# Second convolution of a residual block: a unit's two outer rows placed next to each other, odd weight regions moved by 528 elements

## The chip, the cores and the metric

The kernel runs on one core of a Trainium2 chip. The metric is the device time of one execution in microseconds (us), and lower is better. A run list gives the time of several executions; the profile describes one execution of its own.

## What is computed

A residual block of a diffusion network for two images of 512 channels and 64 x 64 pixels. Two 3 x 3 convolutions with 512 inputs and 512 outputs hold nearly all of the work:

```python
h = conv3(_silu(gn(x, g1, be1)), w1)
emb = _silu(t_emb) @ w_emb
h = h + emb.reshape(B, C, 1, 1)
h = conv3(_silu(gn(h, g2, be2)), w2)
return x + h
```

`gn` is a group norm over four groups of 128 channels. `conv3` pads by one pixel and sums nine taps, each a 512 x 512 product over the channels. Inputs and output are bf16; the kernel keeps intermediate data in fp16.

## The kernel before

**Units.** Each convolution is cut into chunks: an image (`b`) and half of its rows (`ch`), so four chunks for the first convolution (c = 0 to 3) and four for the second (c = 4 to 7). In a chunk, each of the four tiles of 128 output channels (k = 0 to 3) is one unit. Units are numbered 0 to 31; units 16 to 31 are the second convolution, and units 28 to 31 are its last chunk, c = 7.

**A unit's work.** The rows are transformed so that four output rows come from six row planes, s = 0 to 5 (function `rows_a`, `rows_b` and `prod` make the planes of the next chunk while a chunk is multiplied). Planes 0 to 3 are the inner ones; they are also transformed along the columns and multiplied in two kinds of matmul, `B_mms` and `A_mms`. Planes 4 and 5 are the outer ones. In chunks 4 to 6 they are multiplied by `plain_mms` with the three column taps as they are (matmuls with 512 moving columns); in units 28 to 30 they are multiplied by `C_mms` and `D_mms` (256 columns), for which `outer_weights` (L757) first makes sums and differences of the taps on VectorE. TensorE's results go to PSUM, ScalarE copies them to SBUF (`evac_m`, `evac_b`, and `evac_o` at L838 for the outer planes), VectorE combines the inner planes into four output rows in a buffer `ys`, and the two outer rows are added to the first and last of these. There are two `ys` buffers, for even and odd units.

**How the outer rows are added.** In units 16 to 27 an accumulating DMA issued by GpSimd (POOL) adds them (L1034 to L1038, called the accumulate here): one DMA with two runs of 520 elements per partition, one from each outer row, except that units 16 and 17 use two DMAs of one run each. After it, a second POOL DMA adds the whole of `ys` to the output in HBM (called the output DMA here), to which the input `x` has been copied earlier.

**Where things lie.** One big SBUF tile `ar` holds everything. Its first part is four regions `UREG[0]` to `UREG[3]` of 10,256 elements each. In the second convolution region j holds, from its start, 8,192 elements of inner weights of output tile j (`um1`, L509, filled by `fetch_w2`, L594), then at 8,192 a streamed part of 1,536 elements, then at 9,728 one outer row of 520 elements. The streamed part belongs to no fixed tile: a unit u uses slot s = u mod 2, which is the pair of regions 2s and 2s + 1, and its raw outer weights are loaded in two halves, channels 0 and 1 of the input into region 2s and channels 2 and 3 into region 2s + 1 (`stream_w2`, L605; `st_off`, L512). I call these the even half and the odd half; each is a DMA of 384 KB. The unit's two outer rows lie in the same two regions:

```python
OO = [UREG[2 * (u % 2) + 1] + 9728, UREG[2 * (u % 2)] + 9728]
...
oo = A(OO[1], [[OO[0] - OO[1], 2], [1, PL]])
```

So the accumulate's source (L1028) is one access pattern with two runs, 10,256 elements apart.

**What sets the order.** Every operation is recorded by a planner and then emitted in the order of a fixed list (`ORDER`, `emit`), so each engine and each DMA queue has one fixed order. SyncE (SP) issues all plain loads and stores (helper `dma`, L385), in order: a load that waits holds all that stand behind it. POOL issues the accumulates, the output DMAs and some small memsets, in order as well. The planner knows the exact elements of each access. The waits that the chip sees are not the planner's: the framework below adds them when the operations are emitted, from the access patterns of the one tile `ar`. In the built program of before, the odd half of a unit's streamed weights (nine of the sixteen odd halves) waits for an accumulate of an earlier unit of the same slot, and nine accumulates wait for an odd half that was loaded; the even halves have no such wait, although they lie next to an outer row in the same way.

**The place that matters below.** SP issues, in this order: the odd half of unit 27 and some more; then the odd half of unit 28, its even half, the even half of unit 29, a part of `x` for the last unit, the odd half of unit 29; later the even and odd halves of units 30 and 31. The odd half of unit 28 waits for the accumulate of unit 26, of unit 24, and for the last matmul of unit 26 that reads the old odd half. VectorE reads the new half in `outer_weights`.

All vector additions are recorded by one helper and stand under L347, scalings on VectorE under L351, ScalarE's work under L370, matmuls under L400 and DMAs under L385.

Of the kernel before, what the change touches and what calls it, by code (L numbers as in the profile page):

```python
# [14 lines left out]
BF16 = mybir.dt.bfloat16  # L15
# [100 lines left out]
def _idx(off, dims):  # L116
    idx = np.array([off])
    for s, c in dims:
        idx = (idx[:, None] + (np.arange(c) * s)[None, :]).reshape(-1)
    return idx  # L120
# [3 lines left out]
RW = 65  # L124
# [13 lines left out]
CFG = {  # L138
    'k0': ('DVE', 'DVE', 'DVE', 'DVE'),
    't0': 'DVE',  # L140
    'k': ('DVE', 'DVE', 'DVE', 'ACT', 'ACT', 'ACT', 'DVE', 'ACT'),
    't': ('DVE', 'DVE', 'DVE', 'DVE', 'ACT', 'ACT', 'ACT', 'DVE'),
    's': (('DVE', 'DVE', 'DVE'), ('DVE', 'DVE', 'DVE'), ('DVE', 'ACT', 'ACT'), ('DVE', 'DVE', 'DVE'), ('ACT', 'ACT', 'ACT'), ('ACT', 'ACT', 'DVE'), ('ACT', 'ACT', 'ACT'), ('DVE', 'ACT', 'DVE')),
    'st1': (1, 1, 1, 1),
    'oacc': (4, 4, 4, 0, 4, 4, 4, 0),
    'ym': (1, 1),
# [14 lines left out]
    'embat': -1,  # L161
    'aacc': (0, 0, 0, 0, 0, 0, 0, 0),
    'embk': 1,
}


# [54 lines left out]
def kernel(  # L221
# [15 lines left out]
    UREG, UM = [], 10256  # L237
# [57 lines left out]
    def K(*k):  # L295
        if k not in keys:
            keys[k] = len(keys)
        return ("K", np.array([keys[k]]))

    def A(off, dims, dt=None):  # L300
        b = ar[:] if dt is None else ar[:].bitcast(dt)
        n = 1
        for d in dims:
            n *= d[1]
            assert d[1] == 1 or -32768 <= d[0] <= 32767
        return R(bass.AP(b.tensor, b.offset + off, [list(b.ap[0])] + [list(d) for d in dims]),
                 ("A", _idx(off, dims)), n)
# [35 lines left out]
    def regs(*rs):  # L343
        return [r.reg if isinstance(r, R) else r for r in rs]

    def tt(out, a, b, op, name=""):
        pl.op("DVE", 0.075 + 0.000521 * out.n, lambda: nc.vector.tensor_tensor(out=out.ap, in0=a.ap, in1=b.ap, op=op),  # L347
              regs(a, b), regs(out), name)
# [31 lines left out]
    def dma(out, in_, r, w, nbytes, name="", sw=False, acc=False, after=None, seq=None):  # L380
        rate = 0.15 if acc else rate0[0]
        kw = {"accum_op": ALU.add, "max_dma_last_dim": 2080} if acc else {}
        eng = nc.gpsimd if sw else nc.sync
        return pl.op("DMA", nbytes / rate * 1e-6 if nbytes > 30000 else 0.1,
              lambda: eng.dma_start(out=out, in_=in_, **kw), regs(*r), regs(*w), name, lat=3.2 if sw else None, after=after, sw=sw, seq=seq)  # L385

    def memz(eng, out, name="", v=0.0):
        e = getattr(nc, eng)
        pl.op("POOL" if eng == "gpsimd" else "DVE", 0.08 + 0.0005 * out.n, lambda: e.memset(out.ap, v), (), regs(out), name)  # L389
# [116 lines left out]
    def ur0(j, ct, ky, kx):  # L506
        return A(UREG[j] + 7168 + ct * 768 + ky * 384 + kx * 128, [[1, 128]], BF16)

    def um1(j, ct, kx, pos):  # L509
        return A(UREG[j] + ct * 2048 + kx * 512 + pos * 128, [[1, 128]])  # L510

    def st_off(s, ct):  # L512
        return UREG[2 * s + ct // 2] + 8192 + (ct % 2) * 768

    rawc = [0]

# [76 lines left out]

    def fetch_w2(j):  # L594
        nm = f"f2_{j}"
        d = A(UREG[j], [[2048, 4], [1, 1536]])
        dma(d.ap, u_scr[j], [K("u", j, c) for c in range(CT)], [d], P * 4 * 3072, nm)
        for c in range(0, CT, 2):
            g = lambda kx: A(UREG[j] + c * 2048 + kx * 512, [[2048, 2], [1, 512]])
            t = A(TB, [[512, 2], [1, 512]])  # L600
            tt(t, g(0), g(2), ALU.add, nm)
            tt(g(3), t, g(1), ALU.add, nm)
            tt(g(1), t, g(1), ALU.subtract, nm)

    def stream_w2(s, j):  # L605
        for h in range(2):
            d = A(UREG[2 * s + h] + 8192, [[1, 1536]], BF16)
            dma(d.ap, w2[j][:, h * 1536:(h + 1) * 1536], [], [d], P * 3072, f"st_{j}")


# [2 lines left out]
    def nst(c):  # L613
        return CFG["nst"][c] if c < 4 else 4
# [142 lines left out]
    def outer_weights(sl, k):  # L757
        nm = f"ow{k}"
        for h in range(2):
            g = lambda kx: A(UREG[2 * sl + h] + 8192 + kx * 128, [[384, 4], [1, 128]], BF16)  # L760
            t = A(VB[0] + 6144 + h * 512, [[1, 512]])
            cd = ND[k] + h * 1024
            tt(t, g(0), g(2), AD, nm)
            tt(A(cd, [[1, 512]]), t, g(1), AD, nm)
            tt(A(cd + 512, [[1, 512]]), t, g(1), SB_, nm)
# [48 lines left out]
    def unit(c, k, opening=0):  # L814
        l, b, ch = chunks[c]
        md = mode(c)
        u = ucnt[0]
# [5 lines left out]
        M = lambda i, n=1, st=512: A(MB + i * 512, [[st, n], [1, 512]]) if n > 1 else A(MB + i * 512, [[1, 512]])  # L823
        if md == "1":
            BT, SD = BT1, SD1
            OO = [UREG[2 * (u % 2) + 1] + 9728, UREG[2 * (u % 2)] + 9728]
        else:
            BT, SD = BT0, SD0
            OO = [O0[2 if u == 2 else u % 2] + PL, O0[2 if u == 2 else u % 2]]
        if l == 0 and ch == 0 and b not in SSUM:  # L830
# [7 lines left out]
        def evac_o(s, bank):  # L838
            act(A(OO[s - 4], [[RW, 8], [33, 2], [1, 32]]), Ps(bank, 0, [[1, 512]]), fid,
                scale=(0.25, 1.0)[s - 4], acc=acc(s), name=nm + f"o{s}")  # L840
# [118 lines left out]
        elif c == 7 and CFG["no"]:  # L959
# [13 lines left out]
            g = lambda q: A(NB_ + q * 256, [[512, 2], [32, 8], [1, 32]])  # L973
# [39 lines left out]
        if last:  # L1013
# [6 lines left out]
            for r0, n, i in ((1, 2, None), (3, 1, 0), (0, 1, 1)):  # L1020
                if i is not None:
                    tt(seg(ot, r0, 1, BF16), seg(ys, r0, 1), A(OO[i], [[1, PL]]), AD, nm + "O")
                o_ = seg(ot, r0, n, BF16)
# [3 lines left out]
        yo = A(ys, [[24 * RW, 2], [1, PL]])  # L1027
        oo = A(OO[1], [[OO[0] - OO[1], 2], [1, PL]])  # L1028
        if c == 7 and CFG["no"]:
            for i in range(2):  # L1030
                yr = A(ys + i * 24 * RW, [[RW, 8], [33, 2], [1, 32]])
                tt(yr, yr, A(NB_ + 2560 - i * 512, [[1, 512]]), AD, nm + "O")
        elif k < CFG["oacc"][c] and c == 4 and k < 2:
            for i in range(2):  # L1034
                y_, o_ = A(ys + 24 * RW * i, [[1, PL]]), A(OO[1 - i], [[1, PL]])
                dma(y_.ap, o_.ap, [o_, y_], [y_], P * 2 * PL, nm + "oa", sw=True, acc=True)
        elif k < CFG["oacc"][c] and not last:
            dma(yo.ap, oo.ap, [oo, yo], [yo], P * 4 * PL, nm + "oa", sw=True, acc=True)  # L1038
        else:
            tt(yo, yo, oo, AD, nm + "O")  # L1040
# [157 lines left out]
    for ct in range(CT):  # L1198
        d = A(XB0[ct], [[1, AF]], BF16)
        dma(d.ap, x[0, ct, 0], [], [d], P * AF * 2, f"x0{ct}", seq=seq)  # L1200
        d = A(XB1[ct], [[1, YF]], BF16)
# [69 lines left out]
    for c in range(8):  # L1271
        l, b, ch = chunks[c]
        for k in range(CT):
            if c == 0:
                if k + 1 < CT:
                    if k == 2:
                        load_ur(3)
                    prep_w1(k + 1, "ACT", [WS, E0[0], E0[1], TB])
                if k == CFG["embk"]:
                    emb()  # L1280
            if c == CFG["np"]:
                nest_w1(k)
            if c < 4 and nst(c) == 3 and nst(c - 1) != 3:
                nest_w1b(k)
            for i in range(CFG["w2d"][c][k]):
                prep_w2(w2n[0] // 4, w2n[0] % 4)
                w2n[0] += 1
            if c == 4 and k == 0:
                for j in range(CT):
                    memz("gpsimd", A(UREG[j] + 9728 + 32, [[RW, 8], [1, 1]]), "oz")  # L1290
            if l == 1:
                stream_w2(ucnt[0] % 2, k)
                if c == 7 and k < 3 and CFG["no"]:
                    outer_weights(ucnt[0] % 2, k)
                for i in range(2 if ucnt[0] < 31 else 0):
                    r0, r1 = i * YF // 2, (i + 1) * YF // 2
                    dma(out[b, k, ch][:, r0:r1], x[b, k, ch][:, RW + r0:RW + r1], [], [K("o", b, k, ch, i)],
                        P * YF * 1.4, f"pre{c}{k}", after=ufirst[max(ucnt[0] - CFG["pre"], 0)])
            run_later = list(later)
            later.clear()  # L1300
            unit(c, k, opening=2 if c == 0 and k < 3 else 0)
            for f in run_later:
                f()
            if c == 0:
                stats1(k)
            if c == 1:
                if k == CFG["st1at"]:
                    gn_chain(0, 1, 0, [(ME1, 0, 2 * CT)], "st1", n=CT)
                for q in range(CT):
                    if k == max(CFG["st1at"], min(q + CFG["st1at"], CT - 1)):  # L1310
                        prod(2, q)
            elif c + 1 < 8:
                prod(c + 1, k)
            if c == 3:
                fetch_w2(k)
# [71 lines left out]
```

## Time and profile before

| what | us |
| --- | --- |
| median of 3 runs (lowest to highest) | 467.13 (466.95 to 468.02) |
| the profiled execution, its time | 466.26 |
| the profiled execution, its span | 464.5 |
| TensorE (PE) matmuls busy | 447.6 (96% of the span) |
| VectorE (DVE) busy | 440.9 (95%) |
| ScalarE (ACT) busy | 377.0 (81%) |
| GpSimd (POOL) busy | 65.8 (14%) |

The span is the time from the first to the last instruction of the program in the trace; the profiled execution's own time is 1.76 us longer. Two engines are busy for nearly all of the span, so an average says little: what counts is where either of them stands still. A line of the timeline reads: start, length, engine, source line, operation, what is written and read, how many instructions are merged into the line, and in square brackets the idle time before it and what ended that. A line of the waits reads: engine, what was waited for, the sum of the time, the number of waits, the longest. SPq is SP's queue of DMA issues. The granted clock (PEclk) is 1.00 when TensorE runs at full speed. DMAs of the profile's list of issues are given with the time from issue to landing.

### The profile page before, as it was taken

The page shows a single profiled execution, that of the slowest core. Times are in us where ns is not written, and L with a number is a line of the kernel's source. Part 1 is how long each engine was busy: PE and PEld are TensorE (multiplying, and loading weights), DVE is VectorE, ACT ScalarE, POOL GpSimd, SP SyncE. Part 2 cuts the span into 40 slices and gives each one's busy share as a digit, 9 for nine tenths or more (in the row PEclk, how much of TensorE's full clock was granted, in tenths as well). Part 3 has the DMA queues.
Part 4 walks back from the last instruction along what each step waited for, and adds up shares of the span by engine and source line. Part 5 has one row for each costly group of instructions (what it writes and reads, how often), then busy time and mean ns, then how long its engine had stood idle before and what let it go on. Part 6 is the DMA issues. An engine that isn't in the chain of part 4 may idle for free. (4 is left out here: it accounts for less than half of the span.)

```text
span 464.5 us, 8112 instructions
## 1 busy us (share of the span) xinstructions
PE 447.6 (96%) x2891; PEld 281.5 (61%) x2891; DVE 440.9 (95%) x842; ACT 377.0 (81%) x571; POOL 65.8 (14%) x91
## 2 busy tenths in 40 slices
PE   8999999999999999999999999999999999959995
PEld 5744344465554666566556766657776677747882
DVE  4899999999999999999999999999999999949995
ACT  5899999987958999998999898757868798726572
POOL 2210010211021111011000002122221231211210
PEclk9999999999999999999999999999999999998999
DMA  8955682697649387686977687779789777495744
GB/s 314 381 215 168 177 220 71 179 270 212 216 103 295 85 254 230 190 254 198 355 263 275 213 290 177 187 188 195 184 215 268 215 173 180 70 222 136 163 76 92
DMA packets 44472, 94.89 MB, mean 204 GB/s; under 512 B 6544, under 2 KB 18192, under 8 KB 44432
## 3 DMA queue, kind: packets, MB, share of 16 engines
q1 hardware_dynamic: 32208, 77.60, 49.4%
q0 software_dynamic: 11936, 16.78, 23.5%
q8 instruction: 22, 0.36, 0.3%
q14 instruction: 18, 0.15, 0.1%
q10 hardware_dynamic: 288, 0.01, 0.0%
HBM read 62.25 MB, written 31.32 MB: 201 GB/s over the span
## 5 line engine op out<-in xcount | busy, mean ns | idle before, releaser
L400 PE MATMUL psum<-ar 128*128 128x256 f16 (+2 forms) x2771 | 429.7, 317 | 9.6 <-ACT ar L370 5.4
L347 DVE TENSOR_TENSOR ar<-ar 128x1040 f16<-128x1040 f16 (+8 forms) x621 | 409.0, 716 | 12.6 <-DMA ar<-in_w_dram 6.5
L400 PEld LDWEIGHTS <-ar 128*128 128x128 f16 (+1 forms) x2763 | 269.0, 98 | 166.8 <-issue 14.9
L370 ACT ACTIVATE ar<-psum 128x512 f16<-128x512 f32 (+4 forms) x250 | 158.9, 679 | 42.6 <-DVE ar L347 21.9
L370 ACT ACTIVATE ar<-ar 128x512 f16<-128x512 f16 (+6 forms) x146 | 158.9, 1116 | 31.3 <-DVE ar L347 26.6
L370 ACT ACTIVATE ar<-ar,fs 128x2112 f16<-128x2112 bf16 (+1 forms) x32 | 68.8, 2150 | 4.3 <-DVE fs L497 1.9
L385 POOL DMA_DIRECT2D ar<-ar x35 | 38.7, 1126 | 196.6 <-DVE ar L347 80.8
L351 DVE TENSOR_SCALAR ar<-ar 128x512 f16<-128x512 f16 (+3 forms) x90 | 31.4, 370 | 0.4 <-issue 0.2
L385 POOL DMA_DIRECT2D out_dram<-ar x15 | 19.0, 1266 | 55.1 <-DMA ar<-ar 30.0
L370 ACT ACTIVATION_READ_ACCUMULATOR ar<-psum 128x1 f32 x104 | 22.3, 214 | 0.0
L389 POOL MEMSET ar<- 128x65 f16 (+4 forms) x29 | 5.3, 216 | 116.0 <-DVE ar L347 76.8
L400 PEld LDWEIGHTS <-ones_bf 128*128 128x128 bf16 x75 | 7.5, 105 | 6.2 <-issue 3.7
L400 PE MATMUL psum<-ar,ones_bf 128*128 128x260 bf16 x56 | 7.3, 275 | 0.7 <-DMA ar<-in_x_dram 0.7
L400 PE MATMUL psum<-ones_bf 128*128 128x512 bf16 x19 | 6.8, 501 | 1.1 <-DVE ones_bf L404 1.1
L370 ACT ACTIVATION_READ_ACCUMULATOR ar<-ar 128x1 f32 x36 | 7.3, 202 | 0.0
L478 POOL TENSOR_TENSOR fs<-fs 128x1 f32<-128x1 f32 x4 | 3.7, 915 | 17.9 <-DVE fs L476 17.9
L400 PEld LDWEIGHTS psum<-fs,ones_neg 128*128 128x128 f32 x36 | 4.7, 191 | 1.6 <-ACT ar L370 1.0
L400 PE MATMUL psum<-fs,ones_neg 128*128 128x1 f32 (+3 forms) x36 | 4.7, 242 | 0.4 <-ACT ar L370 0.4
L400 PE MATMUL psum<-ar,s_sb 128*2 128x512 bf16 x9 | 2.7, 377 | 0.0
L438 ACT ACTIVATE s_sb<-tparm 128x18 bf16<-128x18 bf16 x1 | 0.2, 219 | 3.0 <-DMA tparm<-in_t_emb_dram 3.0
L432 ACT ACT_TABLE_LOAD x1 | 1.3, 1283 | 1.7 <-PEq L1371 1.7
L437 DVE CAST fs<-gparm 128x16 f32<-128x16 bf16 x1 | 0.2, 174 | 2.5 <-DMA gparm<-in_params_dram 2.5
(54 smaller groups left out, 25.5 us busy)
## 6 DMA issues: line engine op xcount, KB each, us to landing
ar<-in_w_dram SPq DMA_DIRECT2D x36, 384.0 KB, 4.4
ar<-in_x_dram SPq DMA_DIRECT2D x16, 552.5 KB, 4.4
h_scr<-ar SPq DMA_DIRECT2D x16, 520.0 KB, 3.8
ar<-h_scr SPq DMA_DIRECT2D x16, 520.0 KB, 4.4
ar<-ar POOLq DMA_DIRECT2D x31, 260.0 KB, 4.5
out_dram<-in_x_dram SPq DMA_DIRECT2D x30, 260.0 KB, 5.3
out_dram<-ar POOLq DMA_DIRECT2D x15, 520.0 KB, 7.2
ar<-in_x_dram SPq DMA_DIRECT2D x13, 520.0 KB, 6.3
```

The source lines that it names most:

```text
L347: pl.op("DVE", 0.075 + 0.000521 * out.n, lambda: nc.vector.tensor_tensor(out=out.ap, in0=a.ap, in1=b.ap, op=op), regs(a, b), regs(out), name)
L351: pl.op("DVE", cost or 0.075 + 0.00026 * out.n, lambda: nc.vector.tensor_scalar(out=out.ap, in0=a.ap, scalar1=s, scalar2=None, op0=ALU.mul ...
L370: lambda: nc.scalar.activation(out=out.ap, in_=a.ap, func=func, scale=sc, **kw), regs(*rr), regs(*ww), name)
L385: lambda: eng.dma_start(out=out, in_=in_, **kw), regs(*r), regs(*w), name, lat=3.2 if sw else None, after=after, sw=sw, seq=seq)
L389: pl.op("POOL" if eng == "gpsimd" else "DVE", 0.08 + 0.0005 * out.n, lambda: e.memset(out.ap, v), (), regs(out), name)
L400: nc.tensor.matmul(out.ap, lhsT=lhsT.ap, rhs=rhs.ap, start=st, stop=sp, skip_group_check=True)
L432: nc.scalar.activation(out=fs[:, WARM:WARM + 1], in_=fs[:, WARM + 1:WARM + 2], func=ACT.Silu)
L437: nc.vector.tensor_copy(out=fs[:, GB:GB + 4 * CT], in_=gparm[:])
L438: nc.scalar.activation(out=s_sb[:], in_=tparm[:], func=ACT.Silu)
L478: pl.op("POOL", 0.85, lambda: nc.gpsimd.tensor_tensor(out=F(rs, n).ap, in0=N.ap, in1=F(NEGH, n).ap, op=ALU.pow), regs(N), regs(F(rs, n)), ...
```

## The change

Odd regions (j = 1 and 3) are laid out the other way around: the outer row comes first, at the region's start, and the inner weights and the streamed part follow 528 elements on. Region 2s still ends with its outer row, at 9,728 to 10,248, and region 2s + 1 begins at 10,256, so the two outer rows of a slot now lie 528 elements apart in place of 10,256, with 8 elements between them and nothing of another kind in between. The two runs of the accumulate, its bytes and its addresses in `ys` stay. All weight addresses of odd regions go through `um_off`; the zeroing of a pad column of the outer rows follows the new place. A constant in the condition of the split accumulates becomes an entry of the table with the same value.

```diff
+    'split4': 2,
...
+    def um_off(j):
+        return UREG[j] + 528 * (j % 2)
+
     def um1(j, ct, kx, pos):
-        return A(UREG[j] + ct * 2048 + kx * 512 + pos * 128, [[1, 128]])
+        return A(um_off(j) + ct * 2048 + kx * 512 + pos * 128, [[1, 128]])

     def st_off(s, ct):
-        return UREG[2 * s + ct // 2] + 8192 + (ct % 2) * 768
+        return um_off(2 * s + ct // 2) + 8192 + (ct % 2) * 768
...
     def fetch_w2(j):
         nm = f"f2_{j}"
-        d = A(UREG[j], [[2048, 4], [1, 1536]])
+        d = A(um_off(j), [[2048, 4], [1, 1536]])
         dma(d.ap, u_scr[j], [K("u", j, c) for c in range(CT)], [d], P * 4 * 3072, nm)
         for c in range(0, CT, 2):
-            g = lambda kx: A(UREG[j] + c * 2048 + kx * 512, [[2048, 2], [1, 512]])
+            g = lambda kx: A(um_off(j) + c * 2048 + kx * 512, [[2048, 2], [1, 512]])
...
     def stream_w2(s, j):
         for h in range(2):
-            d = A(UREG[2 * s + h] + 8192, [[1, 1536]], BF16)
+            d = A(um_off(2 * s + h) + 8192, [[1, 1536]], BF16)
...
     def outer_weights(sl, k):
         nm = f"ow{k}"
         for h in range(2):
-            g = lambda kx: A(UREG[2 * sl + h] + 8192 + kx * 128, [[384, 4], [1, 128]], BF16)
+            g = lambda kx: A(um_off(2 * sl + h) + 8192 + kx * 128, [[384, 4], [1, 128]], BF16)
...
         if md == "1":
             BT, SD = BT1, SD1
-            OO = [UREG[2 * (u % 2) + 1] + 9728, UREG[2 * (u % 2)] + 9728]
+            OO = [UREG[2 * (u % 2) + 1], UREG[2 * (u % 2)] + 9728]
...
-        elif k < CFG["oacc"][c] and c == 4 and k < 2:
+        elif k < CFG["oacc"][c] and c == 4 and k < CFG["split4"]:
...
             if c == 4 and k == 0:
                 for j in range(CT):
-                    memz("gpsimd", A(UREG[j] + 9728 + 32, [[RW, 8], [1, 1]]), "oz")
+                    memz("gpsimd", A(UREG[j] + (0 if j % 2 else 9728) + 32, [[RW, 8], [1, 1]]), "oz")
```

Built, the two programs have the same instructions in the same order on every engine and queue. They differ in addresses and in waits. The nine odd halves no longer wait for accumulates, and the nine accumulates no longer wait for odd halves. Eight output DMAs get waits on copies of `x` to the output that the accumulate ahead of them, in the same queue, used to imply. The odd halves of units 16 and 17 wait for matmuls three places later, one VectorE addition for a matmul two places later, and one memset on POOL for a matmul 25 places later.

## The prediction

> **What bounds the kernel now.** I read the slices first, then the table of stages around the hole they show, then the timelines of the engines in it and of the queue of loads, and last the chain.
>
> ```profile
> ## 2 busy tenths in 40 slices
> PE   8999999999999999999999999999999999959995
> ...
> DVE  4899999999999999999999999999999999949995
> ...
> PEclk9999999999999999999999999999999999998999
> ```
>
> TensorE and VectorE are both full until slice 35 (406 to 418 us), and there both drop to half at once. So until then neither can be helped by removing a wait, and the hole is what can be won. The stages (time and busy us of each engine, granted clock, DMA share):
>
> ```profile
> 400.00:409.00 9.00, 7.78 (x66) 6.20 (x65) 9.00 (x15) 5.92 (x8) 2.42 (x2) 1.00 0.31 36
> 409.00:415.00 6.00, 4.27 (x40) 3.68 (x38) 0.12 (x2) 0.00 (x0) 1.19 (x1) 1.00 0.98 236
> 415.00:421.50 6.50, 3.70 (x19) 2.69 (x19) 6.50 (x13) 2.60 (x4) 0.00 (x0) 0.74 0.91 264
> ...
> 425.80:454.00 28.20, 28.17 (x258) 25.10 (x258) 26.34 (x51) 19.55 (x27) 5.22 (x5) 1.00 0.65 124
> ```
>
> VectorE works 9.00 of 9.00 us before 409, 0.12 of 6.00 after it, and again all of 6.50. TensorE stops later and loses twice: it idles, and then runs at a mean clock of 0.74. From 425.8 TensorE is full. The timelines say who waited for whom:
>
> ```profile
> 407.76 1.34 DVE L347 TENSOR_TENSOR ar<-ar 128x1024 f16<-128x1024 f16 x2
> 414.98 3.10 DVE L347 TENSOR_TENSOR ar<-ar 128x512 f16<-128x512 bf16 x5 [5.88 <-DMA ar<-in_w_dram]
> ```
>
> ```profile
> 381.22 1.16 SPq L385 DMA_DIRECT2D out_dram<-in_x_dram x2
> 409.06 1.40 SPq L385 DMA_DIRECT2D ar<-in_w_dram  x3
> ```
>
> ```profile
> SPq L385 <- DMA ar<-ar: 26.6, 2, 16.1
> ```
>
> VectorE's first addition on raw weights (`outer_weights` of unit 28, the bf16 one) waits 5.88 us for a load. SP issued nothing between 382.4 and 409.06; the waits of that stretch give 26.6 us to accumulates (ar<-ar). The load at 409.06 is unit 28's odd half, and it landed 5.8 us later, at 414.9. POOL's timeline has unit 26's accumulate issued at 404.89 (after its rows were ready); it took 4.1 us, to 409.0. That is the chain: accumulate, load, VectorE, ScalarE (idle for 9.02 us to 416.73), TensorE.
>
> ```profile
> 408.53 4.75 PE L400 MATMUL psum<-ar 128*128 128x256 f16 x42 [1.22 <-DVE ar L347]
> 417.80 4.73 PE L400 MATMUL psum<-ar 128*128 128x256 f16 x23 [4.53 <-ACT ar L370]
> 422.89 9.32 PE L400 MATMUL psum<-ar 128*128 128x256 f16 x82 [0.36 <-DVE ar L347]
> ```
>
> ```profile
> 421.24 3.44 DVE ar L347 x6
> ...
> 424.76 1.03 ACT ar L370
> ...
> 425.83 28.12 PE psum L400 x256
> ```
>
> The last is the chain that ended last: VectorE to 424.7, one ScalarE copy, then 256 matmuls without a gap, then the tail. Its VectorE part began in the hole.
>
> **The change, part by part.** Instructions stay; waits go. Matching each wait with the time at which the trace's counters reached its value, I ask what holds each load next.
>
> *Unit 28's odd half* keeps its wait for unit 26's last matmul on the old half. That is the last of twelve 512-column matmuls and ends at 389.08; the load of eight DMAs before it landed at 375.98. So it goes at 389.1 in place of 409.06: 20.0 us earlier. Behind it in SP's queue, the even half goes at 389.5; unit 29's even half waits for a matmul that ends at 400.07 (now 410.03), the `x` part follows at 400.5 (410.57), unit 29's odd half after a matmul at 401.41 (411.07). The slowest of these five took 10.7 us, under the heaviest traffic. With that, unit 28's halves land by 400.2, 9 us before VectorE wants them at 409.02. Unit 29's odd half lands by 412.1; VectorE wants it at 426.46, or 420.5 if it runs 5.96 earlier.
>
> *VectorE* then goes on at 409.02 instead of 414.98 (consecutive additions overlap by 0.08, hence 409.10 less 0.08): **5.96 us**. I checked the 18 additions from there to 424.66 one by one for another wait. ScalarE's inputs were done by 407.71 or follow VectorE itself. The row buffer of unit 27 needs unit 25's output DMA (landed 412.63; wanted 417.50). None binds, so this piece moves whole.
>
> *TensorE* must follow. It ends its work at 413.27, and has 23 matmuls before the one at 422.89, which waits for VectorE; at the pace of the later row (28.12 us / 256 = 0.110) they take 2.5 us, to 415.8. VectorE releases that one at 422.84 - 5.96 = 416.88. So TensorE still waits 1.1 us for VectorE and is not the limit, if its clock is full. In the trace it was not: (1 - 0.74) x 6.50 = 1.7 us of the stage were lost to the clock, right after the 4.53 us of idling; the 1.22 us gap at 407 is followed by 1.00. The remaining gaps are of the second kind. The Trainium skill, TensorE: Matmul & The Clock Gate, section Why this matters for your kernels, advises no idle gaps over about 3 us between bursts; by that rule the clock stays full and the sum is 5.96, while a clock halved for the same 1.7 us would put TensorE 0.6 us behind VectorE and leave about 5.3.
>
> *Later.* Unit 30's loads go after matmuls of unit 28 (425.38 and 426.22) and move along; they landed 3.0 and 2.4 us before use, and both ends move. Unit 28's rows need unit 26's output DMA (421.16, wanted at 426.3), unit 29's need unit 27's (437.67, which follows from the moved chain; slack 4.2 stays). The 256 matmuls and the tail move whole.
>
> *The other eight odd halves*: units 22, 25, 26 and 27 go 1.4, 1.6, 2.1 and 2.6 us earlier, bounded by the matmul that each still waits for; units 23 and 24 are held by SP's queue, unit 31 by TensorE; unit 29 is above. I cost them at nothing: between 315 and 400 no idle time of VectorE or TensorE was ended by a load, so nothing is won, and the cover is that both are full. *The nine accumulates*: each was last released by VectorE, ScalarE or its predecessor; the closest is unit 27 (load 421.74, VectorE 424.66). Nothing. *The eight waits on copies of `x`*: those had landed 60 us or more before. Nothing. *The waits moved by a few matmuls*: at most 2.9 us, and the loads are wanted much later, the addition ran 30 us after that matmul, the memset 35. Nothing.
>
> Sum: 5.96 us. Span 464.5 to 458.5; the profiled execution 466.26 to 460.3. That execution lies 0.87 below the median of the runs shown, so on the median 467.13 - 5.96 = **461.2**.
>
> **The price not shown: traffic.** At 389 to 392 unit 24's accumulate is still in flight, and ScalarE waits for it:
>
> ```profile
> 392.89 1.09 ACT L370 ACTIVATE ar<-psum 128x512 f16<-128x512 f32 x2 [1.00 <-DMA ar<-ar]
> ```
>
> Two loads will now start in its last 3.8 us (it landed at 392.87). Bound from below: none, since it took 11.1 us already under others' traffic, which has thinned out by 391. From above: unit 26's output DMA took 11.8 us beside the five loads, that of unit 24 took 5.9 beside one accumulate, so the excess of 5.9 us. TensorE's next use of that PSUM bank has 0.67 us of slack, VectorE's next input from ScalarE 1.56. I take 1 us, near the lower end because the bytes are nearly through: no loss on VectorE's path. The Trainium skill, DMA: Bandwidth & Descriptors, section Issuing engines are not separate DMA queues, speaks against the change here: DMAs started by different engines run on the same 16 DMA engines and interleave. The 11.8 against 5.9 agrees; by the rule alone the second rival below would be the case to expect, 463.6.
>
> **The rivals.**
>
> *TensorE becomes the bound.* If its clock drops all the same, or work I take for movable isn't, only its idle time comes back: 4.53 + 0.36 = 4.9, time 462.2. For: it is full from 425.8 on. Against: the 1.1 us computed above.
>
> *The loads slow the accumulates.* Unit 24's slips by 3 to 4: VectorE loses 4 - 1.56 = 2.4, gain 3.5, time 463.6. For: ScalarE's wait above. Against: 391 to 393 is nearly idle on the DMA engines.
>
> *Slower.* The old waits kept loads out of the accumulates' way: unit 26's, unit 27's and unit 28's odd halves now start inside units 22's, 23's and 24's. Those of units 22 and 24 are the ones that ScalarE waits on with under 0.2 us of slack. If both took the full 5.9 more, and the first has the second's 0.67 of slack, 2 x (5.9 - 0.67) = 10.5 would be lost on TensorE against 5.96 won: 467.13 + 4.5 = 471.6. It decides from a summed slip of 6 us past the slack. Against: the bytes are the same, and traffic moved forward leaves 409 to 421 emptier.
>
> *It doesn't do what it says.* Another wait holds VectorE at 409 anyway: 467.1. Against: the even half, the next candidate, waits for nothing later than 377.8.
>
> **How the numbers follow.** Forecast 0.72; TensorE 0.09; slowed accumulates 0.11; no effect 0.04; slower 0.04. Predicted 461.2. The range goes from 459.6 (the profiled execution's 460.3, less 0.7 for thinner traffic) to 463.6 (the second rival). A difference under 0.3% (1.4 us) can't be told from none. Faster by more: 0.92; within: 0.04; slower: 0.04.
>
> **What would show it.** SP issues unit 28's odd half near 389 and the three behind by 402. VectorE has no wait for a load near 409. The 4.53 us gap of TensorE is gone, with under 1.3 us in its place, and the clock reads 1.00 throughout until the tail. ScalarE's wait near 393 stays under 2 us. The last 256 matmuls start near 420. If that start moves less, the first step late after 409 tells which rival holds; it is wrong altogether if a stall of about 6 us stands elsewhere.

## The result and the profile after

| | before | after |
| --- | --- | --- |
| median, run side by side (lowest to highest), us | 467.57 (466.95 to 470.03), 4 runs | 461.24 (460.51 to 461.67), 4 runs |
| ratio of the times, 95% interval | | 0.9853 [0.9814, 0.9892] |
| profiled execution, its time / span, us | 466.26 / 464.5 | 461.67 / 459.9 |
| spans of the four runs after, us | | 458.7, 459.2, 459.8, 459.9 |

The change is faster by 1.5%, 6.3 us between the medians; the prediction was 5.96 us and 461.2. That the median hits 461.2 to a tenth is partly luck: the four runs before spread over 3.1 us and the four after over 1.2, and 5.96 was taken off a median of 467.13, not of 467.57. What carries the reading is the step of 5.96 us found in the traces below. The profile after is that of the slowest of its four runs. All line numbers after are one higher (additions L348, ScalarE L371, DMAs L386, matmuls L401), since the change adds a line above them.

The slices of the profile after, in the order in which those of before were read:

```profile
PE   8999999999999899999999999999999999989995
...
DVE  4899999989999999999999999999999999999995
...
PEclk9999999999999999999999999999999999999999
```

The common drop of TensorE and VectorE in slice 35 is gone, and with it the dip of the clock. SP's queue from 390 us, and VectorE's waits from 270 us to the end, after:

```profile
390.44 11.32 SPq L386 DMA_DIRECT2D ar<-in_w_dram  x3
...
402.76 29.46 SPq L386 DMA_DIRECT2D ar<-in_w_dram  x5
```

```profile
DVE ar L348 <- ACT ar L371: 2.3, 2, 2.0
```

The queue that stood until 409.06 now goes on at 390.44 with unit 28's odd half; the unit's even half and unit 29's even half are the other two of the three merged issues (390.82 and 401.43). VectorE's list of waits has lost its load: what is left are two waits for ScalarE, at 437 and 450 us, and both were there before. The stages around the former hole, with their bounds after 400 shifted by 1.4 us against those of before for a reason given below (time, then busy us of PE, PEld, DVE, ACT, POOL, granted clock, DMA share, GB/s):

```profile
400.00:410.40 10.40, 9.18 (x73) 6.86 (x71) 10.40 (x18) 6.01 (x9) 2.42 (x2) 1.00 0.65 158
410.40:416.40 6.00, 6.00 (x58) 5.37 (x56) 6.00 (x13) 2.43 (x3) 1.19 (x1) 1.00 1.02 171
416.40:422.90 6.50, 5.63 (x48) 4.45 (x46) 6.50 (x15) 4.46 (x8) 1.22 (x1) 1.00 0.15 31
```

VectorE is full in all three, TensorE loses 1.2 and 0.9 us in the first and third, and the clock stays at 1.00. The DMA traffic, which was 36 GB/s from 400 to 409 and then 236 and 264 GB/s, is now spread ahead: 158, 171, and 31. TensorE's timeline names the gaps:

```profile
409.85 7.04 PE L401 MATMUL psum<-ar 128*128 128x256 f16 x63 [1.22 <-DVE ar L348]
417.27 0.61 PE L401 MATMUL psum<-ar 128*128 128x256 f16 x2 [0.38 <-DVE ar L348]
418.24 9.98 PE L401 MATMUL psum<-ar 128*128 128x256 f16 x88 [0.36 <-DVE ar L348]
```

The 1.22 us gap was there before (at 407). The 4.53 us gap has shrunk to 0.38, and the 0.36 ahead of the third row is also old. The chain that ended last, after:

```profile
416.58 3.44 DVE ar L348 x6
...
421.18 28.12 PE psum L401 x256
```

It is the same chain, 4.65 us earlier in this execution.

**Why 4.65 and not 5.96.** Already at 99 us, in the first convolution, this execution fell behind by more than a microsecond. VectorE after, and ScalarE after and before, in the same place:

```profile
99.04 3.70 DVE L348 TENSOR_TENSOR ar<-ar 128x768 f16<-128x768 bf16 x6 [1.33 <-ACT ar L371]
```

```profile
98.49 0.52 ACT L371 ACTIVATE ar<-ar 128x384 bf16<-128x384 bf16 x1 [1.88 <-DMA ar<-in_w_dram]
```

```profile
96.80 0.52 ACT L370 ACTIVATE ar<-ar 128x384 bf16<-128x384 bf16 x1 [0.27 <-DMA ar<-in_w_dram]
```

A weight load of the first convolution came late (7.7 us from issue to landing, 6.1 before), ScalarE waited 1.88 us for it where it had waited 0.27, and VectorE waited 1.33 us for ScalarE. From 102 us on VectorE runs 1.2 us behind before. At its scaling ahead of the former hole it is 1.32 us, the last 0.1 of it from a wait at 354 us (see the traffic below); before and after:

```profile
404.44 0.30 DVE L351 TENSOR_SCALAR ar<-ar 128x520 f16<-128x520 f16 x1
```

```profile
405.77 0.30 DVE L352 TENSOR_SCALAR ar<-ar 128x520 f16<-128x520 f16 x1
```

At the former wait VectorE stands at 410.35 against 414.98, so it gained 4.64 + 1.32 = 5.96 us there. That the late load belongs to the execution and not to the layout is seen in a kernel with the same layout below (unit 28's halves later in the queue), where the same ScalarE line waits 0.24 us, and the changed kernel's own four spans differ by 1.2 us.

### The profile page after: what moved, and what is told of

It is laid out like the page before. It is cut to its first block, busy times and chain, and to the rows that moved or that the text cites. A ratio compares the mean times of both kernels' runs of the same rounds, so it can differ in the third digit from the quotient of the medians.

```text
span 459.9 us, 8113 instructions
## 1 busy us (share of the span) xinstructions
PE 445.3 (97%) x2891; PEld 280.4 (61%) x2891; DVE 440.9 (96%) x842; ACT 377.3 (82%) x571; POOL 65.8 (14%) x91
## 5 line engine op out<-in xcount | busy, mean ns | idle before, releaser
L401 PE MATMUL psum<-ar 128*128 128x256 f16 (+2 forms) x2771 | 427.7, 316 | 6.8 <-DVE ar L348 4.4
L348 DVE TENSOR_TENSOR ar<-ar 128x1040 f16<-128x1040 f16 (+8 forms) x621 | 409.0, 717 | 7.6 <-ACT ar L371 4.2
L401 PEld LDWEIGHTS <-ar 128*128 128x128 f16 (+1 forms) x2763 | 268.1, 98 | 163.0 <-issue 11.7
L371 ACT ACTIVATE ar<-psum 128x512 f16<-128x512 f32 (+4 forms) x250 | 158.7, 679 | 34.8 <-DVE ar L348 16.4
L371 ACT ACTIVATE ar<-ar 128x512 f16<-128x512 f16 (+6 forms) x146 | 158.9, 1116 | 32.3 <-DVE ar L348 26.0
L371 ACT ACTIVATE ar<-ar,fs 128x2112 f16<-128x2112 bf16 (+1 forms) x32 | 68.8, 2151 | 6.1 <-DVE fs L498 3.0
L386 POOL DMA_DIRECT2D ar<-ar x35 | 38.2, 1111 | 193.0 <-DVE ar L348 78.1
L386 POOL DMA_DIRECT2D out_dram<-ar x15 | 19.0, 1265 | 52.6 <-DMA ar<-ar 27.2
L371 ACT ACTIVATION_READ_ACCUMULATOR ar<-psum 128x1 f32 x104 | 22.2, 213 | 0.0
L401 PEld LDWEIGHTS <-ones_bf 128*128 128x128 bf16 x75 | 7.3, 103 | 6.2 <-issue 3.5
L401 PE MATMUL psum<-ar,ones_bf 128*128 128x260 bf16 x56 | 7.3, 275 | 1.1 <-DMA ar<-in_x_dram 0.9
L401 PE MATMUL psum<-ones_bf 128*128 128x512 bf16 x19 | 6.3, 466 | 1.1 <-DVE ones_bf L405 1.1
L371 ACT ACTIVATION_READ_ACCUMULATOR ar<-ar 128x1 f32 x36 | 7.3, 201 | 0.0
L401 PEld LDWEIGHTS psum<-fs,ones_neg 128*128 128x128 f32 x36 | 4.7, 191 | 1.8 <-ACT ar L371 0.9
L401 PE MATMUL psum<-fs,ones_neg 128*128 128x1 f32 (+3 forms) x36 | 4.7, 244 | 0.3 <-ACT ar L371 0.3
L401 PE MATMUL psum<-ar,s_sb 128*2 128x512 bf16 x9 | 2.7, 377 | 0.0
```

The source lines that it names most:

```text
L371: lambda: nc.scalar.activation(out=out.ap, in_=a.ap, func=func, scale=sc, **kw), regs(*rr), regs(*ww), name)
L401: nc.tensor.matmul(out.ap, lhsT=lhsT.ap, rhs=rhs.ap, start=st, stop=sp, skip_group_check=True)
```

## Experiments

**The theory.** One false wait is the whole gain: the wait of unit 28's odd half, the load at the head of SP's queue, for the accumulate of unit 26. It exists because the accumulate's two runs span the streamed part that lies between them. **The rivals**: the gain is a sum over the nine accumulates and odd halves; the two outer rows are read faster when they lie near each other; or the loads must start some 20 us early. The ratios below are against the kernel before, run on the same chip in turns with the kernel in question. The kernel before ran at a median of 466.28 us beside experiments 1 to 4 and at 467.06 beside 5 and 6, against 467.57 above; the expectations in absolute times are therefore a little high.

**1. and 2. The change in one slot only.** Region 1 (even units, with unit 28) or region 3 (odd units) is shifted, and the other odd region stays as before. The edit is against the changed kernel.

```diff
-        return UREG[j] + 528 * (j % 2)
+        return UREG[j] + (528 if j == 1 else 0)
...
-            OO = [UREG[2 * (u % 2) + 1], UREG[2 * (u % 2)] + 9728]
+            OO = [UREG[2 * (u % 2) + 1] + (0 if u % 2 == 0 else 9728), UREG[2 * (u % 2)] + 9728]
...
```

The second kernel has `j == 3` and `u % 2 == 1` there.

> The change made in region 1 alone, so for the units with an even number (slot 0, with units 26 and 28); region 3 stays as before. One-wait theory (the gain is the wait of unit 28's odd half on unit 26's accumulate): all of the gain, a time within 1 us of the changed kernel, 461 to 462, no wait of VectorE for a load near 410. Many-waits theory (the removed waits add up): four of the nine loads are freed, so about 4/9 of 6 us, 464 to 465. Place theory (the nearness of the two rows or the addresses of odd weights matter by themselves): half of the gain, about 464.

> The change made in region 3 alone, so for the units with an odd number (slot 1); region 1 stays as before. One-wait theory: none of the gain, 467 to 468, the hole of 5 to 6 us of VectorE near 409 to 415 stands as before, though five odd halves are free and unit 29's even half can't pass unit 28's in the queue. Many-waits theory: five ninths, about 464. Place theory: half, about 464.

Measured: region 1 alone 460.91 us against 466.28, ratio 0.9874 [0.9849, 0.9899]; region 3 alone 466.29 against 466.28, ratio 0.9997 [0.9981, 1.0012]. With region 1 alone VectorE has no wait for a load, and SP's queue goes on at 390.24:

```profile
390.24 11.32 SPq L386 DMA_DIRECT2D ar<-in_w_dram  x3
```

and SP and VectorE with region 3 alone:

```profile
409.22 1.39 SPq L386 DMA_DIRECT2D ar<-in_w_dram  x3
```

```profile
414.76 5.65 DVE L348 TENSOR_TENSOR ar<-ar 128x512 f16<-128x512 bf16 x11 [5.61 <-DMA ar<-in_w_dram]
```

The even units have all of the gain. The odd units' waits are gone in the second kernel too, and its hole stands nearly unchanged: 5.61 us of waiting for the same load, against 5.88. So the gain is no sum over the nine.

**3. The rows stay far apart, and nothing lies between them.** The inner weights stay where they were; behind them the odd region has its outer row first and then the streamed part. The two rows are 8,720 elements apart instead of 528, with inner weights between them, which no load writes at that time. The edit is against the kernel before.

```diff
-        return UREG[2 * s + ct // 2] + 8192 + (ct % 2) * 768
+        return UREG[2 * s + ct // 2] + 8192 + 528 * (ct // 2) + (ct % 2) * 768
...
-            OO = [UREG[2 * (u % 2) + 1] + 9728, UREG[2 * (u % 2)] + 9728]
+            OO = [UREG[2 * (u % 2) + 1] + 8192, UREG[2 * (u % 2)] + 9728]
...
```

> The outer row of an odd region lies between its inner weights and its streamed part: the two rows of a slot are 8,720 elements apart, the inner weights of odd regions stay where they were, the streamed part goes 528 elements on. The stretch from the first to the last element of the accumulate's source then holds inner weights, which no later load writes, but not the streamed part. Theory that waits come from that stretch: the same nine loads are free and the time is that of the changed kernel, 461 to 462. Place theory (rows side by side matter by themselves, for the accumulate's reads): near 467, or the part of the gain that the addresses of the streamed part give.

Measured: 460.97 us, ratio 0.9877 [0.9853, 0.9902]. In its profile SP goes on at 389.40, and VectorE has no wait for a load:

```profile
389.40 11.32 SPq L385 DMA_DIRECT2D ar<-in_w_dram  x3
```

Nearness is not the cause. In these kernels what counts is only what lies from the first to the last element of the accumulate's source.

**4. The layout of before, and one accumulate as two DMAs.** Only unit 26's accumulate is cut into its two runs, each a DMA of its own, so that neither spans the streamed part. One more DMA goes through POOL; no address changes. The edit is against the kernel before.

```diff
+        elif c == 6 and k == 2:
...
+                for y_, o_ in lst:
+                    nc.gpsimd.dma_start(out=y_.ap, in_=o_.ap, accum_op=ALU.add, max_dma_last_dim=2080)
...
```

> The layout of before; only unit 26's accumulate is issued as two DMAs of one run each, so that neither stretch covers streamed weights. One DMA more on GpSimd. One-wait theory: unit 28's odd half goes when unit 24's accumulate has landed (393 in place of 409), the hole is gone, 461 to 462. Many-waits theory: one wait of nine, under 1 us, 466 to 467. If the two smaller accumulates cost GpSimd or ScalarE time that reaches the end: 1 to 2 us more than the changed kernel.

Measured: 460.73 us, ratio 0.988 [0.9853, 0.9906]. POOL's accumulate as two DMAs and SP's queue:

```profile
404.89 1.77 POOL L1042 DMA_DIRECT2D ar<-ar  x2 [9.79 <-DVE ar L351]
```

```profile
392.39 8.09 SPq L385 DMA_DIRECT2D ar<-in_w_dram  x3
```

Removing this one wait, without any change to the layout, brings the whole gain. The accumulate of unit 26 is issued at 404.89, as before, so it is the load's wait that matters, not one of the accumulate. The load still waits for the accumulate of unit 24, which landed at 392.33, so it goes 3.3 us later than by the matmul (389.1), and that costs nothing. In this execution there is next to no offset from the first convolution (0.05 us), so the step can be read against before directly: the addition at the end of the chain ends at 418.74 in place of 424.66, 5.92 us earlier. The extra POOL DMA is not seen in the time.

**5. The changed kernel with unit 28's halves at the end of the group.** In SP's queue the two halves of unit 28 stand behind those of unit 29. The edit is against the changed kernel; its line numbers are 25 higher (additions L373, DMAs L411).

```diff
...
+        move, last = st[0][-2:], st[1][-1]
+        move.sort(key=seq.index)
+        queue = [i for i in seq if self.ops[i].eng == "DMA" and not self.ops[i].sw and i not in move]
+        at = queue.index(last) + 1
+        queue[at:at] = move
...
```

> The changed kernel with unit 28's two halves moved behind unit 29's two halves and the part of x in SP's queue, so they go at about 403.2 in place of 390.4. In the changed kernel's trace the three DMAs that go first landed at 404.7, 406.0 and 407.1, 1.1 to 1.3 us apart, so these two should land near 408.3 and 409.5; VectorE wants them at 410.35 and 411.9. Theory (VectorE needs the odd half by 410 and nothing else matters): 461, within 0.5 us of the changed kernel, no wait for a load. Rival (what counts is how early the loads go, since they then miss the accumulates' traffic): slower than the changed kernel by 1 us or more, or a new wait of ScalarE for an accumulate.

Measured: 460.36 us against 467.06, ratio 0.9861 [0.9838, 0.9883]. SP's queue and VectorE:

```profile
400.09 0.34 SPq L411 DMA_DIRECT2D ar<-in_w_dram  x1
...
401.42 29.47 SPq L411 DMA_DIRECT2D ar<-in_w_dram  x7
```

```profile
404.64 19.45 DVE L373 TENSOR_TENSOR ar<-ar 128x512 f16<-128x512 f16 x36
```

The odd half is issued at 401.80, 12.7 us later than in the changed kernel with its offset taken off, lands at 407.65, and VectorE takes it at 409.01 without a wait. So the gain does not hang on the 20 us: 7.3 were enough, and, as the load takes 5.8 us here and took 5.8 before, some 6 of them were needed to remove VectorE's 5.88. The time was expected within 0.5 us of the changed kernel's; the medians, from two rounds of runs, are 0.9 apart, the ratios to before 0.9861 and 0.9853. This execution had no offset either, and it hits the prediction's sum: span 458.5, time 460.30, against 458.5 and 460.3 forecast.

**6. Units 16 and 17 with one accumulate each.** With the rows of a slot side by side the two units that use two DMAs could use one. The edit is against the changed kernel; the empty operation keeps the place of the second DMA in the fixed order.

```diff
-            for i in range(2):
-                y_, o_ = A(ys + 24 * RW * i, [[1, PL]]), A(OO[1 - i], [[1, PL]])
-                dma(y_.ap, o_.ap, [o_, y_], [y_], P * 2 * PL, nm + "oa", sw=True, acc=True)
+            pl.op("DMA", 0.1, lambda: None, (), (), nm + "oa", sw=True)
+            dma(yo.ap, oo.ap, [oo, yo], [yo], P * 4 * PL, nm + "oa", sw=True, acc=True)
```

> The changed kernel with the accumulates of units 16 and 17 as one DMA of two runs each, as in units 18 to 27; two DMAs fewer on GpSimd, and no new wait on a load. Theory (GpSimd and its DMAs are off the path there): 461, no difference that can be measured. Rival (fewer issues on GpSimd bring units 16 and 17 forward): faster by up to the 1.2 us that the two extra issues take.

Measured: 461.74 us, ratio to before 0.988 [0.9854, 0.9905], which overlaps that of the changed kernel. POOL in this kernel, and in the changed one, for unit 16:

```profile
283.22 1.19 POOL L386 DMA_DIRECT2D ar<-ar  x1 [3.26 <-issue]
```

```profile
283.58 1.76 POOL L386 DMA_DIRECT2D ar<-ar  x2 [3.27 <-issue]
```

POOL saves some 0.6 us of issuing per unit, and is idle for over 3 us ahead of it either way. No difference in the time can be told; a gain or loss of some tenths of a us isn't excluded.

No kernel is measurably faster than the changed one; the five other kernels with the gain lie between 460.36 and 461.74.

## Why the prediction was right, step by step

*Unit 28's odd half.* Right. Forecast 389.1, then 389.5, 400.1, 400.5 and 401.4 for the four behind it; with the 1.3 us of offset taken off, after has 389.1, 389.5, 400.1, 400.6 and 401.5. The halves landed 4.0 and 4.6 us after their issue. Experiments 1 and 2 narrow the gain to the even units, and experiment 4 shows that this wait alone carries it.

*VectorE, 5.96 us.* Right: 5.96 after (offset taken off), 5.92 in experiment 4 (5.97 with its 0.05 of offset), 5.97 in experiment 5 (424.66 against 418.69). No other wait took the place of the old one.

*TensorE follows.* Right in kind, and a little off in size: 1.1 us of waiting for VectorE was forecast, and it is 0.38 + 0.36 = 0.74. The 23 matmuls ahead of the old wait were busy for 2.9 us (7.04 + 0.61 after, less the 4.75 of the 42 that were done before the hole), where 2.5 was computed from the pace of a later row; the wait, too, is split, since the last two of them wait for VectorE as well (the 0.38). The slack of TensorE against VectorE is thus under 1 us, and by it a further saving on VectorE in this stretch would be worth no more than that; no run tests this.

*The clock.* Right. After the 4.53 us gap of before, the granted clock was halved for most of 3.7 us, and was full again before the next gap:

```profile
417.80:421.50 3.70, 3.70 (x19) 2.69 (x19) 3.70 (x9) 1.53 (x3) 0.00 (x0) 0.54 0.78 252
421.50:425.00 3.50, 3.06 (x26) 2.29 (x25) 3.50 (x8) 1.74 (x4) 0.00 (x0) 1.00 0.01 2
```

After the 1.22 us gap, before and after, it reads 1.00. The Trainium skill, TensorE: Matmul & The Clock Gate, section Why this matters for your kernels, sets the advice at gaps over about 3 us. The gaps here fall on its two sides: 4.53, and 4.26 in experiment 2, went with the half clock, and the longest that left it at 1.00 is one of 1.61 us near 150 us in the profile after; no trace has a gap between 1.61 and 4.26. The half clock cost the kernel before nothing: TensorE still waited 0.36 us for VectorE behind it. A count of all that TensorE lost in the hole, idling and clock, gives 4.53 + 0.36 + 1.7 = 6.6 us, too large a gain; the chain through VectorE gave the right one.

*The traffic.* No loss, as forecast, though the 1 us taken for unit 24's accumulate was not even seen. Times from issue to landing, in us, from the DMA records:

| DMA | before | after | experiment 4 | experiment 5 |
| --- | --- | --- | --- | --- |
| accumulate of unit 24 | 11.1 | 9.6 | 10.5 | 9.5 |
| output DMA of unit 24 | 5.9 | 5.9 | 8.2 | 5.8 |
| accumulate of unit 25 | 6.5 | 5.2 | 8.4 | 5.0 |
| output DMA of unit 26 | 11.8 | 6.1 | 6.3 | 5.9 |
| odd half of unit 28 | 5.8 | 4.0 | 3.3 | 5.8 |

After starts its loads inside unit 24's accumulate, and experiment 5 starts them 9 us after it has landed: 9.6 against 9.5. ScalarE's wait for it, 1.00 us before, is gone; its one wait for an accumulate in the second convolution, at 354 us, is 0.3. The third rival named units 22, 23 and 24, inside whose accumulates odd halves now start: these accumulates took 4.4, 7.1 and 11.1 us before and take 4.6, 5.3 and 9.6 after, so they did not slow down by more than 0.2.

That loads can slow such DMAs is what experiment 4 points to, in one execution, where they start at 392.39, just ahead of unit 24's output DMA and unit 25's accumulate: 8.2 and 8.4 in place of 5.8 and 5.0 in experiment 5. The rule cited in the prediction, that DMAs of different engines share the same 16 DMA engines (the Trainium skill, DMA: Bandwidth & Descriptors, section Issuing engines are not separate DMA queues), agrees with these rows. The 2.4 and 3.4 us of experiment 4 fell on DMAs that no computing engine waited for; so the second and the third rival, with their 2.4 us and more lost on VectorE, did not come about.

A small loss of their kind is in the traces: unit 21's accumulate took 6.7 us before and 7.1 after, ScalarE waits 0.3 us for it at 354 us, and VectorE falls 0.1 us further behind there. VectorE loses 0.4, 0.2 and 0.5 us at that place in experiments 1, 3 and 6, and nothing in 2, 4 and 5. Experiments 5 and 6 share the layout, so whether the loads that now go earlier cause this stays open.

*The other eight odd halves and the moved waits at nothing.* Right as a sum: region 3 alone frees five of them, with its share of the moved waits, and is at 0.9997; experiment 4 frees none of the eight and has the whole gain. What each single one is worth was not measured. The four that were forecast to go 1.4, 1.6, 2.1 and 2.6 us earlier went 1.5, 1.6, 2.0 and 2.6 earlier in experiment 5, whose execution has no offset.

*The span.* 458.5 was forecast; 459.9 came in the profiled execution, 458.5 in experiment 5, 458.7 in the best run after. Of the 1.3 us of difference, 1.2 come from a late load at 97 us, in a part that the change does not touch, and 0.1 from the wait at 354 us.

## What to carry to other kernels

Look at what stands at the head of an in-order load queue when two full engines drop together: one wait there holds every load behind it, and here it was that one wait, not the number of waits removed, that carried the gain. Where a framework takes an access pattern from its first to its last element, a pattern of two far runs waits for all that lies between; reordering the regions, or issuing the runs as two DMAs, removes that wait. Price the hole by the engine that the chain goes through, and take a constant offset between two executions off before comparing their late stages.

## What the runs showed of the hardware that was not expected

The same loads and output DMAs got faster when they were spread. Held together and released at 409, the five loads took 5.8 to 10.7 us and the output DMA beside them 11.8; spread over 12 us, the loads took 3.3 to 4.6 and the output DMA 6.1.

One load of the first convolution varies from one execution to another by enough to move the rest: it took 6.1 us in experiment 5 and before, and 7.7 after, ScalarE waited for it 0.24, 0.27 or 1.88 us, and in the last case VectorE ran 1.2 us later from there on. That is some 0.3% of the whole time. The four runs after, of one and the same kernel, differ by 1.2 us.
